# Block-sparse attention into a gated MLP: two first loads on ScalarE's queue, one first cast on GpSimd, and later queries ahead of values and weights

## Chip, cores and metric

The kernel runs on one core of one Trainium2 chip. The metric is device time in microseconds (us) of one execution; the median of three runs is given. Engines are named as in the profile: PE (TensorE, with PEld for its weight loads), DVE (VectorE), ACT (ScalarE), POOL (GpSimd) and SP (SyncE, which issues DMAs).

## What is computed

Inputs are queries, keys and values q, k, v of shape (4 batches, 8 heads, 768 positions, 64), a list of 3 sampled key blocks for each of the 24 query blocks of 32 positions, and the weights of a gated MLP.

```python
scores = scale * np.matmul(q, k.transpose(0, 1, 3, 2))
mask = np.abs(blk_i - blk_j) <= window               # window = 1, blocks of 32
mask = mask | (blk_i == 0) | (blk_j == 0) | (blk_i == n_blocks - 1) | (blk_j == n_blocks - 1)
for qb in range(n_blocks):
    for kb in sampled_blocks[qb]:
        mask[qb * block:(qb + 1) * block, kb * block:(kb + 1) * block] = True
scores = np.where(mask, scores, -1000000000.0)
...
attn_out = np.matmul(attn, v)                        # attn: softmax of scores over keys
# x: (4, 768, 512), the heads side by side
h = np.maximum(x @ w_in, 0.0)
u, v = h[..., :d_ff // 2], h[..., d_ff // 2:]
v_n = (v - mu) / np.sqrt(var + 1e-06)
v_s = np.einsum('ts,bsd->btd', w_spatial, v_n) + b_spatial[None, :, None]
out = (u * v_s) @ w_out
```

## The kernel before

Heads are taken in pairs: pair p holds two heads of one batch, pairs 0 to 3 are the first batch, 16 pairs in all. The keys and queries of a pair are loaded in float32 (`load`, L105), cast to bf16 into a tile `nat` (`cast`, L119), transposed and copied into `kq`, where the 64 rows of a head are followed by 24 rows that carry the block mask, so that one matmul gives the score with its mask. For pairs 0 to 3 PE does the transposes (`head` L301, `tr_first`, `tr_rest`) and DVE the copies; from pair 4 on a DMA transposes.

The main loop runs over slots. In a slot PE multiplies keys with queries into one of two PSUM tiles `ps` (L443 for the first 36 slots, `qk_unit`; L456 behind them, `qk_full`), ACT takes the exponential into `a_all` (L448, L460), and PE multiplies an earlier `a_all` with the values `vv` (L489, L507). Transposes, mask rows, DVE copies and steps of the MLP (L581) are put into slots by a table written by hand (`when`). The first batch is worked in units of a third of the queries: first head 0 and head 1 of pair 0, then the first third (two chunks of 128 queries) of pairs 1, 2 and 3, then the second third of pairs 1, 2, 3, and at last the third one of pairs 0 to 3. So a pair's queries are loaded in two parts: chunks 0 and 1 (`C01`) and later chunks 2 to 5 (`C25`), which `tr_rest` transposes for pair 1 in slot 12, for pair 2 in slot 15 and for pair 3 in slot 18. Pair 0 has parts of its own: head 0 and head 1 apart (`H0`, `H1`), chunks 0 to 3 (`C03`) and 4, 5 (`C45`).

Every engine works its instructions in the order in which the program gives them (the schedule is manual). A DMA is issued by the engine that carries the call, on that engine's own queue: SP by default, ACT with `eng=nc.scalar`. The DMAs share eight completion semaphores in turn, so a DMA whose semaphore is still in use waits for the landing of the DMA eight places before it, and everything behind it on its issuing engine waits with it. Float32 landing tiles are reused: three for keys, four for queries (L107), six for weights.

The beginning, which the change touches, runs so. ACT issues the two loads of head 0's keys (L141, L142), loads its activation table, does a small exponential, and casts the first part of the keys (L251). SP issues the sampled blocks, then head 0's queries, head 1's keys, head 1's queries (L143 to L146), and then the loads of pairs 1 to 3. POOL makes index tiles, casts head 0's queries (L252), then the rest of head 0's keys, head 1's keys, mask rows for another head (L260), head 1's queries, and after that all of pairs 1 to 3, the values (`vv`) and the weights `w_in_t` in the order written at L271 to L359. DVE copies the transposed pieces into `kq` (L219) and the mask rows (L249).

The body of `load` and the order of POOL's casts from slot 0 on:

```python
eng.dma_start(out=st[nm, p][:, hs, cs.start * D:cs.stop * D],
              in_=dram(SRC[nm], p, hs, cs))
...
cast(1, "v", PL)
rows(slice(6, 8), qcols(0), PL)
cast(2, "v", PL)
cast(1, "q", PL, cs=C25)
rows(slice(2, 4), qcols(1), PL)
w_in_cast(0, 0, PL)
w_in_load(1, 3)
cast(3, "v", PL)
w_in_cast(0, 1, PL)
w_in_load(1, 2)
cast(2, "q", PL, cs=C25)
```

Of the kernel before, what the change touches and what calls it, by code (L numbers as in the profile page):

```python
# [17 lines left out]
def _listify(ap: bass.AP) -> bass.AP:  # L18
    t = ap.tensor
    if isinstance(t.shape, tuple):  # L20
        t = dataclasses.replace(t, shape=list(t.shape))
        ap = dataclasses.replace(ap, tensor=t)
    return ap
# [3 lines left out]
def kernel(  # L27
# [16 lines left out]
    nc = tc.nc  # L44
# [44 lines left out]
    def qcols(t0, n=1):  # L89
        return slice(S + t0 * TW, S + (t0 + n) * TW)  # L90
# [4 lines left out]
    def dram(src, p, hs=slice(0, 2), cs=slice(0, NCH)):  # L95
        b, g = divmod(p, NG)
        return src[b, 2 * g + hs.start:2 * g + hs.stop].rearrange(
            "h (p c) d -> p h (c d)", c=NCH)[:, :, cs.start * D:cs.stop * D]

    H0, H1, BOTH = slice(0, 1), slice(1, 2), slice(0, 2)  # L100
    ALLC, C01, C03, C45 = slice(0, NCH), slice(0, TC), slice(0, 2 * TC), slice(2 * TC, NCH)
    C25 = slice(TC, NCH)
    SRC = {"k": k, "q": q, "v": v}

    def load(p, nm, hs=BOTH, cs=ALLC, eng=nc.sync):  # L105
        if (nm, p) not in st:
            st[nm, p] = work.tile([128, 2, S // 2], FP32, tag="gt" if (nm, p) == ("v", 0) else "st_" + nm,  # L107
                                   bufs=1 if (nm, p) == ("v", 0) else 4 if nm == "q" else 3,
                                   name="st_" + nm)
        eng.dma_start(out=st[nm, p][:, hs, cs.start * D:cs.stop * D],  # L110
                      in_=dram(SRC[nm], p, hs, cs))
# [4 lines left out]
    def nat0_view():  # L116
        return nat[0].rearrange("p c h d -> p (c h d)").rearrange("p (h x) -> p h x", h=2)

    def cast(p, nm, eng, hs=BOTH, cs=ALLC):  # L119
        if nm == "v":  # L120
            dst = vv[p % NVV][:, hs, cs, 0:D]
        else:
            if p not in nat:
                nat[p] = work.tile([128, 2 * NCH, 2, D], BF16, tag="nat", bufs=4, name="nat")
            c0 = 0 if nm == "k" else NCH
            dst = nat[p][:, c0 + cs.start:c0 + cs.stop].rearrange("p c h d -> p h c d")[:, hs]
        src = st[nm, p].rearrange("p h (c d) -> p h c d", d=D)[:, hs, cs]
        if p == 0 and nm != "v":
            dst = nat0_view()[:, hs, (c0 + cs.start) * D:(c0 + cs.stop) * D]
            if cs is not C45:  # L130
                dst = dst[:, 0].rearrange("p (i t d) -> p t i d", t=2, d=D)
                src = src[:, 0].rearrange("p (t i) d -> p t i d", t=2)
            else:
                dst = dst.rearrange("p h (c d) -> p h c d", d=D)
        if eng is nc.scalar:
            nc.scalar.activation(out=dst, in_=src, func=AF.Copy)
        else:
            eng.tensor_copy(out=dst, in_=src)  # L138

    samp = const.tile([KR, 2 * NR], I32)  # L140
    load(0,"k",H0,C03,eng=nc.scalar)  # L141
    load(0,"k",H0,C45,eng=nc.scalar)  # L142
    nc.sync.dma_start(out=samp[MR], in_=_listify(sampled_blocks).bitcast(I32))  # L143
    load(0,"q",H0,C03)
    load(0,"k",H1)
    load(0,"q",H1,C03)  # L146


    eq = const.tile([KR, NR + 1, NB], FP32)
# [66 lines left out]
    PL, DV = nc.gpsimd, nc.vector  # L216
# [14 lines left out]
    def w_in_load(u, g):  # L231
        w_load((u, g), moe_w_in[g * 128:(g + 1) * 128, 0 if u else DH:DH if u else DFF])

    def w_in_cast(u, g, eng):
        eng.tensor_copy(out=w_in_t[:, g, 0 if u else DH:DH if u else DFF], in_=wst.pop((u, g)))  # L235
# [8 lines left out]
    def rows(hs, cs, eng=nc.vector):  # L244
        src = kq[MR, 0:1, cs].to_broadcast([NB, hs.stop - hs.start, cs.stop - cs.start])
        if eng is nc.scalar:
            nc.scalar.activation(out=kq[MR, hs, cs], in_=src, func=AF.Copy)
        else:
            eng.tensor_copy(out=kq[MR, hs, cs], in_=src)  # L249

    cast(0, "k", nc.scalar, H0, C03)  # L251
    cast(0, "q", PL, H0, C03)  # L252
    rows(H1, K_)
    load(1, "k")
# [7 lines left out]
    load(2, "q", cs=C01)  # L262
    load(3, "q", cs=C01)
    load(1, "v")
    load(2, "v")
    load(1, "q", cs=C25)
    cast(0, "q", PL, H1, C03)
    for s in range(NVV):
        nc.gpsimd.memset(vv[s][:, :, :, D:VA], 1.0)
    nc.gpsimd.memset(mhalf, -0.5)  # L270
    cast(1, "k", PL)  # L271
    cast(1, "q", PL, cs=C01)
    load(3, "v")
    w_in_load(0, 0)

# [51 lines left out]
    m2()  # L327
    rows(H1, qcols(0, 3))
    w_in_load(0, 1)
    load(2, "q", cs=C25)  # L330
    w_in_load(0, 2)
    load(0, "q", cs=C45)
    w_in_load(0, 3)
# [6 lines left out]
    cast(3, "q", PL, cs=C01)  # L340
    cast(1, "v", PL)
    rows(slice(6, 8), qcols(0), PL)
    cast(2, "v", PL)
    cast(1, "q", PL, cs=C25)
    rows(slice(2, 4), qcols(1), PL)
    w_in_cast(0, 0, PL)
    w_in_load(1, 3)
    cast(3, "v", PL)
    w_in_cast(0, 1, PL)
    w_in_load(1, 2)  # L350
    cast(2, "q", PL, cs=C25)
    w_in_cast(0, 2, PL)
    w_in_cast(0, 3, PL)
    cast(3, "q", PL, cs=C25)
# [538 lines left out]
```

## Time and profile before

| | us |
|---|---|
| runs shown | 209.82, 210.89, 212.28 (median 210.89) |
| profiled execution | 210.49 |
| its span, first to last instruction | 208.7 |
| PE busy | 201.2 (96%) |
| ACT busy | 167.6 (80%) |
| DVE busy | 132.5 (63%) |
| POOL busy | 71.2 (34%) |
| first exponential of the main loop starts | 6.03 |

Times in views count from the span's start. A timeline row gives start, duration, engine, line, operation, tiles out<-in, shapes, count, and in brackets how long the engine stood idle before it and which instruction or DMA released it. Rows named SPq and ACTq are DMA issues. A row of the chain gives start, duration and what held the chain in that time. A row by stretches gives for PE, PEld, DVE, ACT and POOL the busy time with the number of instructions, then PE's granted clock, the busy share of the DMA engines and what they moved in GB/s. Busy times of PE overlap at their ends, because matmuls are pipelined.

### The profile page before, as it was taken

The page shows a single profiled execution, that of the slowest core. Times are in us where ns is not written, and L with a number is a line of the kernel's source. Part 1 is how long each engine was busy: PE and PEld are TensorE (multiplying, and loading weights), DVE is VectorE, ACT ScalarE, POOL GpSimd, SP SyncE. Part 2 cuts the span into 40 slices and gives each one's busy share as a digit, 9 for nine tenths or more (in the row PEclk, how much of TensorE's full clock was granted, in tenths as well). Part 3 has the DMA queues.
Part 4 walks back from the last instruction along what each step waited for, and adds up shares of the span by engine and source line. Part 5 has one row for each costly group of instructions (what it writes and reads, how often), then busy time and mean ns, then how long its engine had stood idle before and what let it go on. Part 6 is the DMA issues. An engine that isn't in the chain of part 4 may idle for free.

```text
span 208.7 us, 5245 instructions
## 1 busy us (share of the span) xinstructions
PE 201.2 (96%) x2107; PEld 127.6 (61%) x2141; DVE 132.5 (63%) x294; ACT 167.6 (80%) x222; POOL 71.2 (34%) x110
## 2 busy tenths in 40 slices
PE   8899999999999999999999999999999999999993
PEld 6588878766666666655565555665556556544441
DVE  6999687878754545484986455376785433567542
ACT  5899899999989989989998888979999787266021
POOL 5588889566573314042065040131020000003000
PEclk9999999999999999999999999999999999999999
DMA  5999999999999999999735597793101324610266
GB/s 140 341 366 347 291 350 222 296 210 298 256 373 220 276 185 315 260 286 342 181 141 113 115 257 171 231 319 86 38 3 21 67 53 85 244 66 0 50 148 254
DMA packets 64139, 41.82 MB, mean 200 GB/s; under 512 B 45172, under 2 KB 58868, under 8 KB 64116
## 3 DMA queue, kind: packets, MB, share of 16 engines
q1 hardware_dynamic: 63540, 40.91, 75.2%
q10 hardware_dynamic: 576, 0.59, 0.9%
q8 instruction: 16, 0.26, 0.5%
q14 instruction: 7, 0.06, 0.1%
HBM read 24.38 MB, written 6.29 MB: 147 GB/s over the span
## 4 chain that ended last, share of the span: by engine, by line
PE 84%; DMA 7%; ACT 2%; issue 2%; SPq 1%; POOL 1%; DVE 1%; ACTq 0%; POOLq 0%
PE ps_moe L581 31%; PE ps L456 22%; PE ps_av L507 12%; PE ps_t L581 8%; PE ps L443 4%; DMA w_f<-in_moe_w_in_dram 4%; PE ps_sc L581 4%; DMA st_k<-in_k_dram 3%; PE ps_av L489 2%; SPq L110 1%; ACT a_all L448 1%; PE ps L290 1%; POOL w_in_t L235 1%; ACT osb L222 0%; PE ps_av L290 0%
## 5 line engine op out<-in xcount | busy, mean ns | idle before, releaser
L460 ACT ACTIVATE a_all<-ps 128x768 bf16<-128x768 f32 x144 | 113.4, 811 | 14.5 <-PE ps L456 8.3
L456 PE MATMUL ps<-kq 88*128 88x384 bf16 x288 | 70.4, 325 | 0.4
L507 PEld LDWEIGHTS <-a_all 128*128 128x128 bf16 x864 | 45.2, 97 | 20.0
L507 PE MATMUL ps_av<-vv,a_all 128*128 128x65 bf16 x864 | 49.8, 193 | 0.0
L456 PEld LDWEIGHTS <-kq 88*128 88x128 bf16 x288 | 27.7, 98 | 29.7
L581 PE MATMUL ps_moe<-w_in_t,xt 128*128 128x512 bf16 x127 | 38.6, 378 | 0.5
L448 ACT ACTIVATE a_all<-ps 128x1024 bf16<-128x1024 f32 x36 | 34.3, 1026 | 2.5 <-PE ps L443 2.0
L581 PE MATMUL ps_moe<-vn,w_spt 128*128 128x512 bf16 x99 | 30.2, 377 | 0.4
L138 POOL CAST nat<-st_k 128x768 bf16<-128x768 f32 (+2 forms) x17 | 13.4, 790 | 43.3 <-DMA st_k<-in_k_dram 41.6
L620 POOL TENSOR_SCALAR std<-mv 128x3 f32<-128x3 f32 (+1 forms) x9 | 2.1, 238 | 60.8 <-DVE mv L617 43.7
L443 PE MATMUL ps<-kq 88*128 88x256 bf16 (+1 forms) x140 | 21.6, 275 | 0.8 <-DVE kq L219 0.3
L653 DVE SCALAR_TENSOR_TENSOR un<-ps_moe,b_col,un 128x512 bf16<-128x512 f32 x18 | 13.4, 747 | 13.5 <-PE ps_moe L581 11.4
L471 DVE RECIPROCAL rc<-ps_av 128x6 f32<-128x6 f32 (+1 forms) x36 | 6.6, 185 | 23.4 <-PE ps_av L507 21.5
L581 PEld LDWEIGHTS <-xt 128*128 128x128 bf16 x192 | 15.5, 98 | 7.6 <-DVE xt L219 0.2
L581 PE MATMUL ps_moe<-w_out_t,gt 128*128 128x512 bf16 x66 | 19.6, 378 | 0.2
L472 DVE TENSOR_TENSOR xn<-ps_av,rc 128x384 bf16<-128x384 f32 (+1 forms) x36 | 18.5, 513 | 1.2
L616 DVE BATCH_NORM_STATS2 stats<-vn 128x6 f32<-128x512 bf16 x24 | 16.4, 684 | 1.3 <-ACT vn L611 0.9
L138 POOL CAST nat<-st_q 128x768 bf16<-128x768 f32 (+2 forms) x21 | 14.7, 705 | 5.9 <-DMA st_q<-in_q_dram 5.8
L219 DVE COPY kq<-tt 64x1536 bf16<-64x1536 bf16 x24 | 14.9, 620 | 1.8 <-DMA tt<-nat 1.5
L443 PEld LDWEIGHTS <-kq 88*128 88x128 bf16 x140 | 12.5, 97 | 4.6 <-DVE kq L219 0.9
L581 PEld LDWEIGHTS <-w_spt 128*128 128x128 bf16 x144 | 11.6, 98 | 5.6
L138 POOL CAST vv<-st_v 128x768 bf16<-128x768 f32 x15 | 13.0, 867 | 4.1 <-DMA st_v<-in_v_dram 2.7
(83 smaller groups left out, 206.1 us busy)
## 6 DMA issues: line engine op xcount, KB each, us to landing
st_v<-in_v_dram SPq DMA_DIRECT2D x16, 384.0 KB, 6.0
st_k<-in_k_dram SPq DMA_DIRECT2D x15, 384.0 KB, 4.6
out_dram<-osb SPq DMA_DIRECT2D x22, 256.0 KB, 2.9
st_q<-in_q_dram SPq DMA_DIRECT2D x12, 384.0 KB, 4.8
ws_f<-in_moe_w_spatial_dram SPq DMA_DIRECT2D x6, 384.0 KB, 9.1
w_f<-in_moe_w_in_dram SPq DMA_DIRECT2D x8, 256.0 KB, 5.9
w_f<-in_moe_w_out_dram SPq DMA_DIRECT2D x4, 256.0 KB, 4.1
st_q<-in_q_dram SPq DMA_DIRECT2D x6, 128.0 KB, 5.9
```

Source lines behind the costliest of these rows:

```text
L138: eng.tensor_copy(out=dst, in_=src)
L219: nc.vector.tensor_copy(out=o, in_=i)
L443: nc.tensor.matmul(out=ps[:, at:at + n * TW], lhsT=kq[:, h, ci * 128:(ci + 1) * 128], rhs=kq[:, h, qcols(t0, n)], start=True, stop=True)
L448: nc.scalar.activation(out=out, in_=ps, func=AF.Exp, scale=0.125)
L456: nc.tensor.matmul(out=ps[:, hf * 512:hf * 512 + HALF], lhsT=kq[:, j % H, ci * 128:(ci + 1) * 128], rhs=kq[:, j % H, S + hf * HALF:S + (hf ...
L460: nc.scalar.activation(out=a_ref["h", j][:, ci, :].rearrange("p (b c) -> p b c", b=2), in_=ps.rearrange("p (b c) -> p b c", b=2)[:, :, 0:H ...
L471: nc.vector.reciprocal(out=rc[:, 0:n], in_=ps[:, :, D:VA])
L472: nc.vector.tensor_tensor(out=out, in0=ps[:, :, 0:D], in1=rc[:, 0:n].to_broadcast([128, n, D]), op=ALU.mult)
L507: nc.tensor.matmul(out=av_ref[j][:, qc, 0:VA], lhsT=a_ref["h", j][:, ci, qc * 128:(qc + 1) * 128], rhs=vv[p % NVV][:, h, ci, 0:VA], start= ...
L581: nc.tensor.matmul(out=ref["ps"][:, 0:w], lhsT=lhs(i), rhs=rhs(i), start=(i == 0), stop=(i == n - 1))
L616: nc.vector.bn_stats(out=stats, in_=self.vn[:, tcc, :])
L653: nc.vector.scalar_tensor_tensor(out=self.un[:, tcc, :], in0=ps, scalar=b_col[:, tcc:tcc + 1], in1=self.un[:, tcc, :], op0=ALU.add, op1=AL ...
```

## The change

Head 1's first keys and queries are loaded by ACT's queue behind its two loads, and no longer by SP. The first part of head 0's keys is cast by POOL, ahead of head 0's queries, and no longer by ACT. Queries `C25` of pair 1 are loaded and cast ahead of the values of pair 2, and those of pair 2 are loaded ahead of the values of pair 3 and cast ahead of the weight (0,0). PE's and DVE's instructions keep their order; ACT loses one cast and gains two DMA issues, all four of which stand ahead of its table load.

```diff
     load(0,"k",H0,C03,eng=nc.scalar)
     load(0,"k",H0,C45,eng=nc.scalar)
+    load(0,"k",H1,eng=nc.scalar)
+    load(0,"q",H1,C03,eng=nc.scalar)
     nc.sync.dma_start(out=samp[MR], in_=_listify(sampled_blocks).bitcast(I32))
     load(0,"q",H0,C03)
-    load(0,"k",H1)
-    load(0,"q",H1,C03)
...
-    cast(0, "k", nc.scalar, H0, C03)
+    cast(0, "k", PL, H0, C03)
     cast(0, "q", PL, H0, C03)
...
     load(1, "v")
+    load(1, "q", cs=C25)
     load(2, "v")
-    load(1, "q", cs=C25)
     cast(0, "q", PL, H1, C03)
...
     cast(1, "q", PL, cs=C01)
+    load(2, "q", cs=C25)
     load(3, "v")
     w_in_load(0, 0)
...
     w_in_load(0, 1)
-    load(2, "q", cs=C25)
     w_in_load(0, 2)
...
     rows(slice(6, 8), qcols(0), PL)
+    cast(1, "q", PL, cs=C25)
     cast(2, "v", PL)
-    cast(1, "q", PL, cs=C25)
     rows(slice(2, 4), qcols(1), PL)
+    cast(2, "q", PL, cs=C25)
     w_in_cast(0, 0, PL)
     w_in_load(1, 3)
     cast(3, "v", PL)
     w_in_cast(0, 1, PL)
     w_in_load(1, 2)
-    cast(2, "q", PL, cs=C25)
```

## The prediction

> **What bounds the kernel now.** I read the page first, then the chain that ended last in order of time, then the timeline of each engine where that chain leaves TensorE (PE).
>
> ```profile
> span 208.7 us, 5245 instructions
> PE 201.2 (96%) x2107; PEld 127.6 (61%) x2141; DVE 132.5 (63%) x294; ACT 167.6 (80%) x222; POOL 71.2 (34%) x110
> PE 84%; DMA 7%; ACT 2%; issue 2%; SPq 1%; POOL 1%; DVE 1%; ACTq 0%; POOLq 0%
> ...
> 26.00:208.00 182.00, 177.60 (x1793) 108.19 (x1822) 111.41 (x233) 145.75 (x197) 52.02 (x65) 1.00 0.75 187
> ```
>
> The page and one row of the view by stretches (columns: PE, PEld, DVE, ACT, POOL busy with counts, clock, DMA share, GB/s). PE is busy 96% of the span, and 177.6 of the 182 us from 26 to 208, at full clock. Behind 26 us nothing but PE's own work sets the pace, and the change moves none of that work: PE and VectorE (DVE) keep their order. So a microsecond won or lost before 26 us should reach the end whole, as long as later loads keep their lead. The non-PE part of the chain (DMA 7%, POOL 1%) lies before 21 us:
>
> ```profile
> 10.72 7.63 DMA w_f<-in_moe_w_in_dram
> ...
> 18.47 0.61 POOL w_in_t L235
> 19.08 0.77 POOL vv L138
> ...
> 20.41 0.57 POOL nat L138
> ...
> 21.02 0.40 PE ps L290 x4
> ```
>
> GpSimd (POOL) casts in the order written: weight (0,0), v of pair 3, weight (0,1), and only then the later queries of pair 2 ("q2 late" below), which PE needs for its transposes at 21.02. The timelines of PE and ScalarE (ACT) show the price:
>
> ```profile
> 20.18 0.41 PE L489 MATMUL ps_av<-vv,a_all 128*128 128x65 bf16 x8
> 21.02 0.40 PE L290 MATMUL ps<-ident,nat 128*128 128x128 bf16 x4 [0.43 <-POOL nat L138]
> 21.48 0.60 PE L443 MATMUL ps<-kq 88*128 88x256 bf16 x4
> 6.03 15.48 ACT L448 ACTIVATE a_all<-ps 128x1024 bf16<-128x1024 f32 x16 [0.57 <-PE ps L443]
> 22.11 5.83 ACT L448 ACTIVATE a_all<-ps 128x1024 bf16<-128x1024 f32 x6 [0.60 <-PE ps L443]
> ```
>
> PE stands 0.43 us for POOL, and ACT, which ran 16 exponentials without a break from 6.03 to 21.51, stands 0.60 us for PE. From 5 to 20 us DVE and ACT are both nearly full:
>
> ```profile
> 5.00:20.00 15.00, 14.07 (x204) 11.37 (x202) 13.89 (x33) 14.14 (x17) 11.11 (x24) 1.00 1.04 351
> ```
>
> DVE works 13.89 of 15 us (33 instructions, so 0.03 us between two), so earlier data inside this stretch buys little, while a late start of DVE's row of copies costs its full length.
>
> **The change, part by part.**
>
> *Later queries ahead of v and weights.* With q2 late cast before weight (0,0), PE's wait at 21.02 goes. PE counts 0.43 us for it; ACT counts 0.60 us, and 0.60 is also 21.02 minus the issue of the last of the 8 matmuls before (20.18 plus 8 steps of 0.03, by 0.41 for 8 with ends overlapping: 20.42). Bounds 0.43 and 0.60; I take -0.55, as ACT's gap is what PE's next product of queries and keys has to fill.
>
> What is late next is v of pair 3, which now stands behind q2 late and weight (0,0) and is read by the 8 matmuls at 20.18.
>
> ```profile
> 15.32 1.03 POOL L138 CAST vv<-st_v 128x768 bf16<-128x768 f32 x1
> 16.82 0.61 POOL L138 CAST nat<-st_q 128x512 bf16<-128x512 f32 x1 [0.47 <-DMA st_q<-in_q_dram]
> 18.47 0.61 POOL L235 CAST w_in_t<-w_f 128x512 bf16<-128x512 f32 x1 [0.37 <-DMA w_f<-in_moe_w_in_dram]
> 18.41 0.41 PE L489 MATMUL ps_av<-vv,a_all 128*128 128x65 bf16 x8
> ```
>
> Weight (0,0) is cast when it lands, near 18.4. Its load now has 262 kB more (q2 late) ahead of it: 0.75 us at 351 GB/s, so the cast starts at 19.2 and v of pair 3 ends near 19.2 + 0.61 + 0.77 = 20.6, 0.4 us too late. Against that, SyncE (SP) issues the whole stream up to 0.93 us earlier (next part): then it is 18.3 and nothing is late. Bounds 0 and +0.42; I take +0.10, since most of the earlier issue should reach this point. The later queries of pair 1 come before 16.82, v of pair 2 later: its cast (15.32 to 16.35), put one query cast of 0.61 us behind, ends near 17, and its first matmuls run at 18.41. That is covered; uncovered it would cost what it lies past 18.41.
>
> *Two loads on ACT's queue.* The SP loop loses two issues, ACT's gains two:
>
> ```profile
> 1.64 0.41 SPq L110 DMA_DIRECT2D st_k<-in_k_dram  x1
> 2.09 0.43 SPq L110 DMA_DIRECT2D st_q<-in_q_dram  x1
> 2.57 0.43 SPq L110 DMA_DIRECT2D st_k<-in_k_dram  x1
> 0.72 0.88 ACTq L110 DMA_DIRECT2D st_k<-in_k_dram  x2
> 1.63 1.28 ACT L163 ACT_TABLE_LOAD   x1 [1.63 <-PEq L877]
> 4.29 0.37 ACT L222 ACTIVATE kq<-mq 24x256 bf16<-24x256 f32 x1 [0.86 <-PE mq L296]
> ```
>
> Pair 1's keys go out at 1.64 instead of 2.57. On ACT two more issues at 0.44 move the table load from 1.63 to 2.5; it ends at 3.8, the small exponential behind it at 4.0, and the first mask copy is due at 4.29 (ACT stood 0.86 us for PE there). So 0; were issues 0.2 us longer, the copies and the first exponential would follow one for one.
>
> Head 1's keys still leave at about 1.62, third on ACT's queue. But behind them the work is tight:
>
> ```profile
> 4.79 0.51 POOL L138 CAST nat<-st_k 128x384 bf16<-128x384 f32 x1 [0.39 <-DMA st_k<-in_k_dram]
> 5.36 0.82 POOL L249 COPY kq<-kq 24x768 bf16<-24x768 bf16 x1
> 6.25 0.49 POOL L138 CAST nat<-st_q 128x256 bf16<-128x256 f32 x1
> 6.58 0.50 PE L303 MATMUL ps<-ident,nat 128*128 128x128 bf16 x5
> 6.51 1.97 DVE L219 COPY kq<-ps 64x128 bf16<-64x128 bf16 x6
> ```
>
> Landing, cast, mask rows, query cast, five transposes, DVE's copies: each starts as the one before ends, so a later landing moves DVE's full stretch. An earlier one gains at most 0.1 us, DVE being busy. What the landing has to share is seen by stretches:
>
> ```profile
> 1.00:2.00 1.00, 1.00 (x10) 1.00 (x11) 0.88 (x7) 0.37 (x1) 1.00 (x4) 1.00 0.20 23
> 2.00:3.00 1.00, 1.00 (x13) 1.00 (x11) 0.93 (x5) 0.99 (x2) 0.64 (x3) 1.00 0.90 259
> 3.00:4.00 1.00, 1.00 (x10) 0.75 (x9) 0.85 (x5) 0.43 (x2) 0.23 (x1) 1.00 0.93 297
> 4.00:5.00 1.00, 1.00 (x7) 0.54 (x6) 0.25 (x1) 0.69 (x2) 0.61 (x3) 1.00 0.66 107
> q1 hardware_dynamic: 154, 0.16, 68.8%
> q10 hardware_dynamic: 140, 0.06, 28.5%
> ```
>
> The last two rows are the DMA view from 2.5 to 3.3 us: packets of SP's queue (q1) and ACT's (q10) run side by side, 154 to 140. So on ACT's queue head 1's 197 kB of keys no longer follow head 0's queries alone but take turns with an equal amount of pair 1's keys. Before, 525 kB had to pass (131 + 66 + 131 + 197), which 23 + 259 + 297 reaches at 3.8; with 197 kB more it is 721 kB. At the old rates 686 are through by 5.0 and the rest at 5.1: 1.3 later. But from 4 to 5 us only 107 GB/s moved, and the earlier issue can fill that: 190 of the 197 kB fit into it at 297. Head 1's queries, behind the keys, take turns in the same way and are next needed at 6.25. Bounds -0.1 and +1.3; I take +0.15, nearest to the row with the idle DMA.
>
> The page "DMA: Bandwidth & Descriptors" of the Trainium skill (Queues, rings and completion order) says that each DMA engine goes round-robin between its queues, packet by packet; the 154 to 140 agrees. Its section Issuing engines are not separate DMA queues says that a second issuing engine saves only sequencer time: by that the move is worth at most the 0.93 us of issue, and the sharing is rival C.
>
> *Keys of head 0 cast on POOL.* POOL stands idle for 0.99 us up to 3.77; its cast of the queries is of the same size.
>
> ```profile
> DMA to landing us min/median/max: 2.2/3.9/6.5
> 3.04 0.40 ACT L136 ACTIVATE nat<-st_k 128x256 bf16<-128x256 f32 x1
> 3.77 0.40 POOL L138 CAST nat<-st_q 128x256 bf16<-128x256 f32 x1 [0.99 <-DMA st_q<-in_q_dram]
> 9.13 0.40 PE L290 MATMUL ps<-ident,nat 128*128 128x128 bf16 x4 [0.31 <-POOL nat L138]
> ```
>
> The first row is of the view of the key tiles: their first load landed 2.2 us after its issue at 0.72, at 2.92. ACT started 0.12 later, held by its table load; POOL, idle, can start at once: -0.05 (0 to -0.1). If the landing slips past 3.37, the query cast slips too. Pair 1's earlier keys take away PE's 0.31 us at 9.13, but ACT and DVE are full there: 0, bound -0.31.
>
> *Sum.* The profiled execution took 210.49 us (span 208.7). -0.55 + 0.10 + 0.15 - 0.05 = -0.35, so 210.1. The shown runs have the median 210.89 (209.82 to 212.28), 0.4 above that execution: 210.5 there. The bounds add up to -0.60 - 0.1 - 0.1 - 0.31 = -1.1 and -0.43 + 0.42 + 1.3 = +1.3.
>
> **The rivals**, by the median.
> A, the forecast: the gap at 21 us closes, the start stays: 210.5. Chance 0.50.
> B, v of pair 3 takes the place of q2 late: PE stands 0.4 us at 20.2 instead of 0.43 at 21.0: -0.55 + 0.42 + 0.1 gives 210.9. For it speaks that weight (0,0) is cast the moment it lands; against it the earlier issue. 0.18.
> C, slower: head 1's keys and queries, taking turns with pair 1's keys, land 1.3 us late: -0.55 + 0.10 - 0.05 + 1.3 = +0.8, 211.7. It decides from 0.5 us of delay on. For it speaks the chain without slack; against it the idle DMA from 4 to 5 us. 0.20.
> D, the earlier stream pays too: the 0.31 us at 9.13 and the rest of the lower bounds, -1.1: 209.8. Against it speaks DVE's full stretch. 0.12.
>
> **How the numbers follow.** 1%, 2.1 us, is about what a measurement of this kernel can tell from no change. No case reaches it alone; the runs shown scatter by 2.5 us. With about 1 us of scatter on a median, D and a tenth of A give faster 0.10; C, A and B together slower 0.15; the rest, 0.75, within 1%. The range takes the bounds (209.8 to 212.2) and 0.6 more below for scatter: 209.2 to 212.2.
>
> **What would show it.** Right: no wait of PE on POOL at 21 us, ACT's exponentials unbroken past 21.5; SP's third issue at 1.64 is pair 1's keys; ACT's table load at 2.5 with the first mask copy still near 4.25; first exponential near 6.0. B shows as a wait of PE L489 for POOL near 20. C shows as head 1's key cast on POOL well past 4.9 and DVE's six copies stretched past 8.5. Wrong altogether: a new wait of PE behind 26 us, or a first exponential past 6.5.

## The result, and the profile after

The kernel after takes 212.85 us (median of 10 runs, 211.93 to 213.10), the kernel before in the same comparison 210.64 (209.47 to 212.33). The ratio is 1.0104, with a 95% interval of 1.0079 to 1.0130: slower by 1.0%, or 2.2 us. The prediction was 210.5 with a range up to 212.2, so the time lies outside of it, and on the other side of no change. Here and below a median takes in every run, while a ratio leaves out runs over 1.5% above the kernel's fastest, so the two need not agree to the last tenth. The profiled execution took 213.09 us with a span of 211.1.

The page of the kernel after, its first rows, the chain, and the granted clock in 40 slices:

```profile
span 211.1 us, 5243 instructions
PE 203.1 (96%) x2107; PEld 129.2 (61%) x2141; DVE 134.3 (64%) x294; ACT 167.6 (79%) x221; POOL 72.8 (34%) x111
PEclk9769999999999999999999999999999999999999
PE 86%; DVE 5%; issue 2%; ACT 2%; DMA 1%; POOL 1%; SPq 0%; ACTq 0%; POOLq 0%
```

The work is the same (PE 203.1 beside 201.2 us, DVE and ACT within 2 us). New are the dip of the clock in the second and third slice (before, all 40 read 9), and that DMA has left the chain (1% beside 7%) while DVE entered it (5% beside 1%). So the wait that the change aimed at is gone, and the views below place what replaced it before 18 us. The view by stretches, for the kernel after and then for the kernel before:

```profile
4.00:5.00 1.00, 0.94 (x9) 0.45 (x7) 0.49 (x2) 0.85 (x3) 0.62 (x2) 1.00 1.03 382
5.00:6.00 1.00, 0.73 (x6) 0.57 (x7) 0.83 (x4) 0.67 (x3) 0.26 (x1) 1.00 1.08 353
6.00:7.00 1.00, 0.70 (x7) 0.45 (x6) 0.91 (x3) 1.00 (x2) 0.94 (x2) 1.00 1.08 389
7.00:8.00 1.00, 0.33 (x3) 0.34 (x4) 0.00 (x0) 0.68 (x1) 0.94 (x10) 0.75 1.07 352
8.00:14.00 6.00, 6.00 (x44) 4.16 (x43) 4.21 (x10) 4.10 (x4) 4.77 (x8) 0.50 0.97 313
14.00:15.00 1.00, 1.00 (x21) 0.86 (x20) 0.20 (x2) 0.48 (x1) 0.78 (x2) 0.84 1.04 354
```

```profile
7.00:8.00 1.00, 0.90 (x8) 0.40 (x5) 0.84 (x3) 1.00 (x3) 0.09 (x3) 1.00 1.05 356
8.00:14.00 6.00, 5.43 (x81) 4.29 (x82) 5.70 (x12) 5.78 (x7) 4.19 (x7) 1.00 1.07 364
```

Here the time went. From 7 to 8 us DVE does nothing at all (before: 0.84) and PE only 0.33. From 8 to 14 us PE is busy throughout, but with 44 matmuls where it ran 81, at a granted clock of 0.50; ACT gets 4.10 us of work done instead of 5.78, DVE 4.21 instead of 5.70. The 0.75 and 0.84 at the two ends put the half clock from 7.5 to 14.3 us.

How it begins is in the DMA view of the kernel after from 4 to 5 us (packets, MB, share) and in its timelines:

```profile
q1 hardware_dynamic: 137, 0.21, 55.2%
q10 hardware_dynamic: 121, 0.18, 47.5%
```

```profile
0.72 1.38 ACTq L110 DMA_DIRECT2D st_k<-in_k_dram  x3
2.64 1.28 ACT L163 ACT_TABLE_LOAD   x1 [2.64 <-issue]
1.65 0.42 SPq L110 DMA_DIRECT2D st_k<-in_k_dram  x1
...
2.87 0.46 POOL L138 CAST nat<-st_k 128x256 bf16<-128x256 f32 x1
5.75 0.51 POOL L138 CAST nat<-st_k 128x384 bf16<-128x384 f32 x1 [1.13 <-DMA st_k<-in_k_dram]
7.21 0.40 POOL L138 CAST nat<-st_q 128x256 bf16<-128x256 f32 x1
...
7.85 0.82 POOL L138 CAST nat<-st_k 128x768 bf16<-128x768 f32 x1
...
7.67 0.40 PE L304 MATMUL ps<-ident,nat 128*128 128x128 bf16 x2 [0.96 <-POOL nat L138]
...
8.10 1.36 DVE L219 COPY kq<-ps 64x384 bf16<-64x384 bf16 x4 [1.13 <-PE ps L304]
```

The hole that the DMA engines had from 4 to 5 us is filled (382 GB/s beside 107), but ACT's queue (q10, head 1's keys) gets 0.18 MB of it and SP's (q1, pair 1's keys) 0.21. Head 1's keys, issued at 1.63 as before, are cast at 5.75, not 4.79. The delay of 0.96 then runs down the chain as the prediction's rows show it: query cast 7.21 (6.25 before), PE's transposes stand 0.96 us for it, DVE stands 1.13 us for PE, and its six copies end at 9.46 instead of 8.48.

ACT's timeline of the kernel after shows the price, and what was won:

```profile
4.26 0.37 ACT L222 ACTIVATE kq<-mq 24x256 bf16<-24x256 f32 x1
5.75 1.94 ACT L448 ACTIVATE a_all<-ps 128x1024 bf16<-128x1024 f32 x2 [0.31 <-PE ps L443]
8.95 1.02 ACT L448 ACTIVATE a_all<-ps 128x1024 bf16<-128x1024 f32 x1 [1.27 <-PE ps L443]
...
14.52 2.87 ACT L448 ACTIVATE a_all<-ps 128x1024 bf16<-128x1024 f32 x3 [0.67 <-PE ps L443]
17.97 12.37 ACT L448 ACTIVATE a_all<-ps 128x1024 bf16<-128x1024 f32 x13 [0.58 <-PE ps L443]
```

The first exponential is 0.28 us earlier (5.75 beside 6.03), and that buys nothing. The third waits 1.27 us, five more wait between 0.26 and 0.67, and the tenth starts at 17.97. In the trace of before, where 16 follow each other from 6.03 on, the tenth starts at 14.96, so this is 3.0 us behind. From there ACT runs 13 without a break; the 0.60 us that it stood at 22.1 before is gone, and 3.0 less 0.6 is the 2.4 us by which the span is longer.

### The profile page after: what moved, and what is told of

It reads as the page before. It is cut to its first block, busy times and chain, and to the rows that moved or that the text cites. A ratio compares the mean times of both kernels' runs of the same rounds, so it can differ in the third digit from the quotient of the medians.

```text
span 211.1 us, 5243 instructions
## 1 busy us (share of the span) xinstructions
PE 203.1 (96%) x2107; PEld 129.2 (61%) x2141; DVE 134.3 (64%) x294; ACT 167.6 (79%) x221; POOL 72.8 (34%) x111
## 4 chain that ended last, share of the span: by engine, by line
PE 86%; DVE 5%; issue 2%; ACT 2%; DMA 1%; POOL 1%; SPq 0%; ACTq 0%; POOLq 0%
PE ps_moe L581 30%; PE ps L456 21%; PE ps_av L507 12%; PE ps_t L581 8%; PE ps L443 7%; PE ps_sc L581 4%; PE ps_av L489 3%; DVE kq L219 1%; DMA st_q<-in_q_dram 1%; PE ps L291 1%; ACT a_all L448 1%; DVE vn L187 1%; DVE kq L249 1%; POOL nat L138 1%; DVE stats L616 1%
## 5 line engine op out<-in xcount | busy, mean ns | idle before, releaser
L456 PEld LDWEIGHTS <-kq 88*128 88x128 bf16 x288 | 27.7, 98 | 29.7
L138 POOL CAST nat<-st_k 128x768 bf16<-128x768 f32 (+3 forms) x18 | 13.9, 773 | 41.7 <-DMA st_k<-in_k_dram 41.5
L443 PE MATMUL ps<-kq 88*128 88x256 bf16 (+1 forms) x140 | 23.8, 294 | 1.1 <-DVE kq L219 0.8
L653 DVE SCALAR_TENSOR_TENSOR un<-ps_moe,b_col,un 128x512 bf16<-128x512 f32 x18 | 13.5, 748 | 13.6 <-PE ps_moe L581 11.3
L138 POOL CAST nat<-st_q 128x768 bf16<-128x768 f32 (+2 forms) x21 | 15.6, 746 | 6.9 <-DMA st_q<-in_q_dram 6.5
L443 PEld LDWEIGHTS <-kq 88*128 88x128 bf16 x140 | 13.2, 102 | 5.1 <-DVE kq L219 1.1
L219 DVE COPY kq<-tt 64x1536 bf16<-64x1536 bf16 x24 | 15.8, 657 | 0.3
L187 DVE TENSOR_SCALAR vn<-ps_moe 128x512 bf16<-128x512 f32 x18 | 12.3, 681 | 3.0 <-PE ps_moe L581 2.7
```

The lines of the kernel that those rows point to most:

```text
L187: nc.vector.tensor_scalar(out=out, in0=in0, scalar1=s1, scalar2=s2, op0=o0, **kw)
L219: nc.vector.tensor_copy(out=o, in_=i)
L443: nc.tensor.matmul(out=ps[:, at:at + n * TW], lhsT=kq[:, h, ci * 128:(ci + 1) * 128], rhs=kq[:, h, qcols(t0, n)], start=True, stop=True)
L456: nc.tensor.matmul(out=ps[:, hf * 512:hf * 512 + HALF], lhsT=kq[:, j % H, ci * 128:(ci + 1) * 128], rhs=kq[:, j % H, S + hf * HALF:S + (hf ...
L653: nc.vector.scalar_tensor_tensor(out=self.un[:, tcc, :], in0=ps, scalar=b_col[:, tcc:tcc + 1], in1=self.un[:, tcc, :], op0=ALU.add, op1=AL ...
```

## The experiments

Each was timed in turn with the kernel before, in four groups, in which its median was 210.69, 210.95, 210.45 and 211.15. In the expectations, L1 is the theory that the halved clock is the price, L2 that it is the delay of head 1's chain itself; S is turns between the two queues as the cause, D the delay of head 1's casts as the price.

**The three parts alone.** Only the two loads on ACT's queue:

```diff
+    load(0,"k",H1,eng=nc.scalar)
+    load(0,"q",H1,C03,eng=nc.scalar)
...
-    load(0,"k",H1)
-    load(0,"q",H1,C03)
```

> Only the two loads of head 1 move to ScalarE's queue. Theory L (the loads do the whole harm: head 1's keys land late, PE stands, and its clock halves for some windows): about 2.8 us slower than before (the change's 2.2 plus the 0.6 that its reordering wins), with head 1's key cast on POOL past 5.5 us and a stretch of granted clock 0.5 behind it. Rival R (the reordering or the POOL cast does the harm): within 0.5 us of before.

Measured: 212.46 us, ratio 1.0073 (1.0041 to 1.0104). Only the new order of the later loads and casts:

```diff
+    load(1, "q", cs=C25)
     load(2, "v")
-    load(1, "q", cs=C25)
...
+    cast(2, "q", PL, cs=C25)
     w_in_cast(0, 0, PL)
```

> Only the later queries of pairs 1 and 2 are loaded and cast earlier. Theory L: 0.5 to 0.6 us faster than before, PE's 0.43 us wait for POOL at 21 us gone, the start as before. Rival R: slower than before by 1 us or more.

Measured: 211.19 us, 1.0024 (0.9992 to 1.0055). Only head 0's keys cast by POOL:

```diff
-    cast(0, "k", nc.scalar, H0, C03)
+    cast(0, "k", PL, H0, C03)
```

> Only the first cast of head 0's keys moves from ScalarE to GpSimd. Theory L: within 0.3 us of before. Rival R (the cast on POOL holds up the start): slower by 0.5 us or more, with the first exponential past 6.3 us.

Measured: 210.57 us, 0.9990 (0.9967 to 1.0014). The kernel with the loads alone has most of the loss, and neither of the other parts a gain that can be told from none. But the loads alone delay more than head 1: ACT, which there still casts the first part of head 0's keys, does so at 4.03 instead of 3.04, behind its two new issues, and the first exponential goes to 6.45. In the whole change POOL has that cast, so 1.0073 isn't the loads' share of 1.0104. The kernel that undoes the loads, below, is the cleaner one.

**Is it the halved clock?** The kernel after with 16 spare matmuls on PE between head 1's key and query transposes.

```diff
+        filler(16, ps1[:, 768:1024].bitcast(FP32))
```

> The changed kernel with 16 small matmuls of zeros (each 128 columns, about 0.055 us, into unused columns of the same PSUM bank) between the key and the query transposes of head 1, where PE stands 0.96 us. The late keys stay. Theory L1 (most of the loss is PE's halved clock behind its idle time): no stretch at clock 0.5 behind 7 us, and about 1.5 to 2 us faster than the changed kernel, so 0.2 to 0.7 us slower than before. Rival L2 (the loss is the delay itself, the clock costs little): within 0.5 us of the changed kernel, so about 2 us slower than before.

Measured: 213.20 us, 1.0117 (1.0069 to 1.0164): no better. Rows of its timelines (POOL, PE, DVE, ACT, and PE near the end):

```profile
6.17 0.67 POOL L138 CAST nat<-st_k 128x384 bf16<-128x384 f32 x1 [1.79 <-DMA st_k<-in_k_dram]
...
7.08 1.06 PE L181 MATMUL ps<-warm 128*128 128x128 bf16 x16
...
10.81 1.07 DVE L138 CAST vv<-st_v 128x768 bf16<-128x768 f32 x1
...
17.15 12.37 ACT L449 ACTIVATE a_all<-ps 128x1024 bf16<-128x1024 f32 x13 [0.99 <-PE ps L444]
...
205.06 1.04 PE L582 MATMUL ps_sc<-w_out_t,gt 128*128 128x512 bf16 x4 [1.26 <-DMA gt<-un]
```

The spare matmuls ran where PE had stood, and those behind them kept full speed (0.60 us at 8.37 for the two of 512 columns that take 1.06 at 7.85 in the kernel after). Still the tenth exponential starts at 17.15, 2.2 us behind that of before and 0.8 ahead of that of the kernel after. The 0.8 us is not the whole price of the half clock: head 1's keys were cast at 6.17 here, 0.42 us later than in the kernel after, so with equal delays the difference would be larger. This execution then lost 1.26 us more near 205 us, where PE waited for a transfer of the last stage (213.91 in all), so the total says less than the stage; without it the span of 212.1 would be 210.8, still 2.1 us above that of before. So in this execution the loss is there at full speed too. How much the half clock adds stays open. DVE's cast of v, which takes 1.07 us here and 0.56 in the kernel before, doesn't explain the rest: in the kernel after itself it takes 0.56 us.

Three of the ten runs of the kernel after show a mean clock of 0.984 and take 213.1; the rest, with a median of 212.7, are slower than before as well. That doesn't settle it, because a mean clock of 1.000 can hide half speed, as the kernel with two spare copies shows below.

**Undoing the loads alone.** The kernel after, with head 1's loads back on SP's queue.

```diff
-    load(0,"k",H1,eng=nc.scalar)
-    load(0,"q",H1,C03,eng=nc.scalar)
...
+    load(0,"k",H1)
+    load(0,"q",H1,C03)
```

> The changed kernel with head 1's two loads back on SyncE's queue: reordering and POOL cast stay. Theory (the loads do the harm; the reordering wins nothing on the median, since a start that is 0.5 us later hides the same wait): within 0.5 us of before. Rival (the reordered casts do harm of their own, as the median of the reordered kernel, 0.5 us over before, hints): 0.4 to 1 us slower than before.

Measured: 211.02 us, 0.9977 (0.9951 to 1.0002). The 1.0% is gone. In POOL's timeline the cast of head 1's keys (second of the two in this row) starts without a wait:

```profile
4.10 0.74 POOL L138 CAST nat<-st_k 128x128 bf16<-128x128 f32 x2
```

**ACT's queue, or the turns?** In the kernel before, head 1's keys stay on SP's queue and pair 1's keys go third on ACT's.

```diff
+    load(1,"k",eng=nc.scalar)
...
-    load(1, "k")
```

> Before, with pair 1's keys as third load on ScalarE's queue; head 1's keys stay on SyncE's queue behind head 0's queries. Theory S (two queues share the DMA engines by turns, so head 1's keys are late because pair 1's keys run beside them): head 1's keys land past 5.2 us although their own queue and place did not change, and the time is 0.8 to 2 us over before. Rival Q (ScalarE's queue, or the third place on it, is slow by itself): head 1's keys land near 4.7 us and the time is within 0.5 us of before.

Measured: 212.20 us, 1.0073 (1.0038 to 1.0108). The time agreed with the theory of turns, the profiled execution didn't: head 1's keys landed at 4.83, their cast stood at 4.88, and that execution was the fastest of the kernel's runs (210.16).

```profile
4.88 0.51 POOL L138 CAST nat<-st_k 128x384 bf16<-128x384 f32 x1 [0.40 <-DMA st_k<-in_k_dram]
```

So the same kernel was run once more.

> A second look at the kernel before with pair 1's keys third on ACT's queue and head 1's on SP's. The first look's profiled execution was the fastest of its runs and had head 1's keys landing at 4.83, while the median was 1.25 us up. If taking turns between the queues is what delays head 1's keys, this execution, if a slow one, has them land past 5.2 and DVE's copies start past 7; if they land at 4.8 again and the span is near 210, the loss in this kernel has another place, to be read from the exponentials.

Measured: 211.99 us, 1.0073 (1.0050 to 1.0095), with an execution near the median (211.97). Its rows from POOL and ACT:

```profile
5.88 0.51 POOL L138 CAST nat<-st_k 128x384 bf16<-128x384 f32 x1 [1.50 <-DMA st_k<-in_k_dram]
...
16.98 9.62 ACT L448 ACTIVATE a_all<-ps 128x1024 bf16<-128x1024 f32 x10 [1.02 <-PE ps L443]
```

In this execution head 1's keys, on the queue that they had before, are late by as much as in the kernel after (5.88 beside 5.75), with pair 1's keys on the other queue. So ACT's queue is not needed for the delay; a second load beside them is enough, though not in every execution of this kernel (4.88 and 5.88). Nor is the share even: from 4 to 5 us of the late execution the DMA view has 199 packets of ACT's queue and 61 of SP's. ACT's third issue also moves its cast of head 0's keys from 3.04 to 3.53, in both executions.

**The delay without the loads.** The kernel before, with two spare copies of mask rows (1.38 us) on POOL ahead of head 1's key cast; then with one (0.82 us).

```diff
     cast(0, "k", PL, H0, C45)
+    rows(slice(3, 4), K_, PL)
+    rows(slice(3, 4), slice(0, 384), PL)
     cast(0, "k", PL, H1)
```

> Before, with two extra copies of mask rows on GpSimd (the same values again, 768 and 384 columns) ahead of head 1's key cast, so that this cast starts at 5.7 us as in the changed kernel, with no load changed. Theory D (the late start of head 1's casts alone makes the loss): 1.2 to 2.2 us over before. Rival B (a good part comes from the other traffic of DMAs at the start): less than 0.7 us over before.

Measured: 212.56 us, 1.0060 (1.0026 to 1.0095).

> The kernel before, with one spare copy of head 3's mask rows (0.82 us) on POOL ahead of head 1's key cast, which comes 0.4 to 0.6 us later than before's 4.79; two such copies brought 1.2 us and 1.6 us of time. Nothing is left out. If the price follows the delay, 0.7 us and a ratio of 1.002 to 1.004; if there is slack up to some 0.5 us, as the prediction's third rival had it, 1.000 within 0.002; if it is a step (PE's idle time halves the clock or doesn't), the full 1.006 or nothing.

Measured: 211.12 us, 1.0006 (0.9976 to 1.0036). The key casts, the first row of the kernel with two copies, the second with one:

```profile
5.97 0.50 POOL L138 CAST nat<-st_k 128x384 bf16<-128x384 f32 x1
```

```profile
5.33 0.50 POOL L138 CAST nat<-st_k 128x384 bf16<-128x384 f32 x1
```

0.54 us later than 4.79 costs nothing that can be measured, and 1.18 us later costs 1.3 us by the ratio (0.5 to 2.0). Whether there is a threshold can't be told from these two points: one for one, 0.5 and 1.2 us, lies inside both intervals. A delay alone, with no load moved, makes a good part of the loss.

What in the delay costs the time isn't separated here. In the execution shown with two copies PE ran at half speed to about 13.6 us, under a mean clock of 1.00:

```profile
11.95 1.06 PE L445 MATMUL ps<-kq 88*128 88x512 bf16 x2
```

**More work on POOL.** The kernel before with one spare cast of pair 1's keys on POOL, behind its casts of pair 1.

```diff
+    spare = const.tile([128, 2, S // 2], BF16, name="spare")
+    nc.gpsimd.tensor_copy(out=spare, in_=st["k", 1])
```

> Before, with one more cast of pair 1's keys on GpSimd into a spare tile (128x768, 0.82 us) in GpSimd's idle time near 9.5 to 10.7 us. Theory P (GpSimd's casts lengthen VectorE's copies that run at the same time, which adds to the loss where the changed kernel moves casts under copies): the cast of v on VectorE (0.56 us before) takes 0.9 us or more and the time is 0.3 to 0.7 us over before. Rival N (no such effect): that cast stays near 0.56 us and the time within 0.2 us.

Measured: 210.93 us, 1.0000 (0.9972 to 1.0028). The spare cast ran from 8.49 to 9.32 and so missed DVE's cast of v (0.56 us, at 9.92): it says that POOL has room there, and nothing on what the two cost each other. Other executions do: the cast of v took 1.07 us in the fastest execution with pair 1's keys on ACT's queue, whose span is 208.1, and 1.20 us with the loads undone (209.4). So a longer cast of v alone doesn't make the 2.4 us.

**Shortening the chain.** The kernel after, with POOL's copy of head 3's mask rows put behind head 1's query cast; then the same with head 1's loads back on SP's queue.

```diff
-    rows(slice(3, 4), K_, PL)
...
     cast(0, "q", PL, H1, C03)
+    rows(slice(3, 4), K_, PL)
```

> The kernel after, with POOL's copy of head 3's mask rows (0.83 us, between head 1's key cast and query cast) put behind the query cast. Nothing is left out. If what is lost comes through head 1's chain (landing, key cast, query cast, transposes, DVE's copies), the query cast can start where the key cast ends or the queries land (6.6 instead of 7.21), PE stands 0.4 us instead of 0.96 there, and 0.6 us or more comes back: 212.0 and a ratio to before of 1.005 to 1.008. If the loss comes from elsewhere (more traffic beside DVE, pair 1's keys cast on POOL earlier), the time stays 212.8, ratio 1.010.

Measured: 212.08 us, 1.0066 (1.0031 to 1.0101): what was expected of the chain, though the interval overlaps that of the kernel after. In the execution shown, one of the two fastest of this kernel, head 1's keys are cast as late as 5.96, but its queries at 6.75 and not at 7.21; DVE's six copies end at 8.89, and the span is 208.9, near that of before.

> The kernel after with head 1's loads back on SP's queue, and POOL's copy of head 3's mask rows behind head 1's query cast. Nothing is left out. It is the best version that the runs so far point to. If POOL's rows copy lies on the chain, the query cast comes up to 0.35 us earlier than before's 6.25 where the queries have landed by then (5.9 in both executions seen), and the ratio to before is 0.995; if the queries' landing binds, as it does in the execution seen of the kernel without this edit (6.03 behind a wait of 0.31), nothing is won: 0.998.

Measured: 211.18 us, 1.0031 (1.0006 to 1.0056). Nothing is won; the query cast stood a full microsecond for its data:

```profile
5.84 0.40 POOL L138 CAST nat<-st_q 128x256 bf16<-128x256 f32 x1 [1.00 <-DMA st_q<-in_q_dram]
```

Without the turns the rows copy has cover, the landing of the queries, and moving it gains nothing. That the kernel came out 0.3% slower is not explained.

**The kernel before once more.**

> The kernel before once more, as a control of the comparison and of what differs between two executions. Ratio 1.000 within 0.003. If full clock begins at another time than 5.1 us and the gap of 0.6 us at 22 us shrinks by what the exponentials start later, the gap is set by when the casts on POOL come, not by their order, and the first part of the prediction's sum could not be won from the median.

Measured: 210.69 us, 1.0010 (0.9979 to 1.0041). Its row of ACT:

```profile
6.37 20.03 ACT L448 ACTIVATE a_all<-ps 128x1024 bf16<-128x1024 f32 x21 [0.91 <-PE ps L443]
```

21 exponentials in one piece: the gap of 0.60 us on which the prediction's first term rested isn't there, with no instruction moved. Nor is it in the kernel with the loads alone, which keeps the old order and has one stretch past 22 us:

```profile
14.58 11.73 ACT L448 ACTIVATE a_all<-ps 128x1024 bf16<-128x1024 f32 x12 [0.44 <-PE ps L443]
```

The second execution of the kernel before started them 0.34 us later and still ended earlier, with a span of 208.1 beside 208.7.

**Taking the turns away, on ACT's queue.** The kernel after, with a small memset by which SP's load of pair 1's keys, and all behind it, waits for POOL's cast of head 0's keys. Its ratio is the lowest of all, but not to be told from the 0.9977 of the kernel that undoes the loads.

```diff
     cast(0, "k", PL, H0, C03)
+    st["k", 1] = work.tile([128, 2, S // 2], FP32, tag="st_k", bufs=3, name="st_k")
+    nc.gpsimd.memset(st["k", 1][:, 0, 0:1], 0.0)
```

> The kernel after, with one small memset on POOL, behind its cast of head 0's keys, into a corner of the tile of pair 1's keys, so that SP's load of them (and all of its later ones) goes out near 3.3 instead of 1.65. Head 1's keys and queries stay on ACT's queue. Nothing is left out. If the turns with pair 1's keys are what makes head 1's keys late, they land at 4.9 or before, their cast stands near 4.9 and the ratio to before is within 0.3% of 1; pair 1's keys, issued 0.8 later than before, land near 8. If it is ACT's queue as such, head 1's keys land at 5.7 again and the ratio stays at 1.007 to 1.013. A loss with head 1's keys on time would be the price of the later stream.

Measured: 210.52 us, 0.9972 (0.9942 to 1.0003). Its issue by SP, then POOL and ACT:

```profile
3.41 0.39 SPq L110 DMA_DIRECT2D st_k<-in_k_dram  x1
...
4.09 0.74 POOL L138 CAST nat<-st_k 128x128 bf16<-128x128 f32 x2
...
6.80 0.82 POOL L138 CAST nat<-st_k 128x768 bf16<-128x768 f32 x1 [0.28 <-DMA st_k<-in_k_dram]
...
6.03 20.97 ACT L450 ACTIVATE a_all<-ps 128x1024 bf16<-128x1024 f32 x22 [0.57 <-PE ps L445]
```

Head 1's two loads are still on ACT's queue, but their keys are cast without a wait, as soon as the cast before is done (two casts in 0.74 us from 4.09). Pair 1's keys, issued 1.76 us later than in the kernel after, land 0.8 us later (6.75 beside 5.96) and are still cast 1.05 us earlier, at 6.80: in the kernel after POOL, behind head 1's late casts, gets to them only at 7.85. ACT runs 22 exponentials without a gap, and the span is 207.8 us. It beats the kernel after clearly (0.9972 beside 1.0104, each against the kernel before); its lead of 0.3% on the kernel before isn't resolved.

## Why the prediction was wrong

**The step that failed** is the term "+0.15" for the two loads on ACT's queue. The mechanism was in the text (its bound of +1.3, and rival C); the value was taken at the wrong end. The DMA engines' idle time from 4 to 5 us was read as room for what pair 1's keys displace. The sum of bytes behind it was loose from the start: it has head 1's keys through at 3.8 us in the kernel before, where their cast waits for the landing until 4.79. The idle time was filled, but in turns: more than half of it went to SP's queue, where pair 1's keys stand first. Head 1's keys came 0.96 us late, against the 0.15 taken. The page "DMA: Bandwidth & Descriptors" of the Trainium skill (Queues, rings and completion order) has the turns packet by packet; the 137 to 121 packets agree, the 199 to 61 of the other kernel with two loads side by side don't. The run that holds SP's load back shows that what runs beside head 1's keys decides.

**The price of the delay** was the second miss, in A and in C alike. C passed it on one for one and came to 211.7. With 0.96 us in place of 1.3 that way of counting gives 0.5 us; measured were 2.2 (1.7 to 2.7). In the kernel after 0.96 us at head 1's casts became 3.0 us at the tenth exponential: DVE stands empty from 7 to 8 us and PE for two thirds of it, and then PE runs at the half clock to 14.3. What each of these is worth is not separated: the one execution that kept full speed was 0.8 us earlier at the tenth exponential, with a longer delay. The two delays made on POOL fit one for one as well as more. C's signs were seen, the key cast well past 4.9 and DVE's copies past 8.5.

**The term -0.55** for the gap at 21 us: in the two profiled executions PE no longer waits there, ACT's 0.60 us are gone, and the 0.6 reached the end whole. But that agreement is not the new order's doing as far as is shown: the gap belonged to the one execution shown before, a second one has none, nor has the kernel with the loads alone in the old order, and the new order alone measured 1.0024 (0.9992 to 1.0055). The kernel that undoes the loads and the one that holds SP's load back (0.9977 and 0.9972) stand near the -0.5 us that the sum makes without its +0.15, neither clear of 1.

**The term +0.10** for v of pair 3 (rival B) was nothing: no wait of PE for POOL stands near 20 us, in a kernel that is 3 us late there. **The term -0.05** had the right sign: POOL cast head 0's keys at 2.87, ACT had at 3.04. **ACT's table load** went to 2.64 and the first mask copy stayed at 4.26, as forecast: 0. **Rival D** fell with the start. The prediction's own sentence that a late start of DVE's row of copies costs its full length points at what happened; the price, 2.2 us, was more than the delay in any execution shown with the loads moved (key casts at 5.75 to 6.17, 0.96 to 1.38 us late).

## What to carry to other kernels

Moving a load to another engine's queue didn't put it ahead here: it put it beside what the first queue sent next. So ask which transfer gains the place, how many bytes it has, and whether a chain without slack waits for the one that loses. Idle time of the DMA engines is not room for the late transfer unless it is the only one left to fill it; holding the less urgent load back by 1.8 us had both cast earlier here. A gap read from one execution is a term only when a second execution has it too.

## What the runs showed of the hardware

The clock halved without a long idle stretch. In the kernel after PE stood 0.96 us at most in one piece and was busy 2.33 of the 3.41 us from 4.05 to 7.46 (before: 3.25, and the clock stayed); from 7.5 to 14.3 us it ran at 0.50. In the execution with POOL's rows copy put behind the query cast the half clock lasted 3.4 us, from 7.4 to 10.8. The 6.8 us of the kernel after are two windows of the 3.4 us that the page "TensorE: Matmul & The Clock Gate" of the Trainium skill gives (What's actually happening); its rule that gaps of over some 3.4 us are what brings the clock down (HAM oscillation — how this bites in real kernels) doesn't cover this case.

When full speed begins differs from execution to execution, and the granted clock doesn't show it. Two matmuls of 512 columns in the run with one spare mask copy, and the row by stretches:

```profile
7.70 1.06 PE L444 MATMUL ps<-kq 88*128 88x512 bf16 x2
```

```profile
7.00:8.00 1.00, 1.00 (x8) 0.79 (x7) 0.46 (x3) 1.00 (x2) 1.00 (x9) 1.00 0.92 314
```

At full speed the same two take 0.59 us (7.10 in the run that holds SP's load back), so this is half speed under a clock of 1.00. By the durations, full speed began by about 5.4 us in some executions and between 8 and 14 in others. Where head 1's keys were cast by 5.4 us, the four executions of the first kind have spans of 207.8 to 208.7 us, and the six of the second, all with full speed by 10 us, 208.8 to 209.8. So a late beginning may cost up to about 1 us; as these are nearly all different kernels with one execution each, that is not shown.
